# Windowed attention, a gated block and a second block on one core: attention of the last seven pieces by units of two groups, and another order of the work

## The chip, the cores and the metric

The kernel runs on one core of a Trainium2 chip as one program. The metric is the device time of one execution in microseconds (us). The engines are named as in the profile: PE (TensorE matmul), PEld (its weight loads), DVE (VectorE), ACT (ScalarE), POOL (GpSimd) and SP (SyncE, which here only issues DMAs).

## The reference

```python
def _attn_ref(q, k, v):                      # 4 x 8 heads x 576 x 64
    scores = np.matmul(q, k.transpose(0, 1, 3, 2)) / np.sqrt(64)
    rel = pos[:, None] - pos[None, :]
    # heads 0-3: 0 <= rel < 32;  heads 4-7: 0 <= rel < 128 and rel % 4 == 0
    scores = np.where(mask, scores, -1e9)
    attn = np.exp(scores - scores.max(-1))
    return np.matmul(attn / (attn.sum(-1) + 1e-9), v)

def _moe_ref(x, w_gate, w_val, w_out, rms_g):   # 2304 x 512, inner width 1536
    xn = x / np.sqrt(np.mean(x * x, -1) + 1e-06) * rms_g
    g = xn @ w_gate
    return (g / (1 + np.exp(-g)) * (xn @ w_val)) @ w_out

def _moe2_ref(x, w_in, w_out, g_ln):            # inner width 1024
    h = x @ w_in;  solu = h * softmax(h)
    return (layer_norm(solu) * g_ln) @ w_out

def reference(q, k, v, ...):  return _moe2_ref(_moe_ref(rows(_attn_ref(q, k, v))))
```

All inputs and the output are float32. The kernel splits each operand of a large product into a high and a low half in a 32-bit matmul type and adds three products (`mm3`, L889 to L892).

## The kernel before

**Tiling.** The 2304 tokens are cut into nine pieces of 256 (`PIECES`). A piece has four groups of attention work, or five (pieces 4 and 8, counted from 0): two of plain heads, and two of dilated heads or, with five, one kind "both" and two "tail". A group holds 8 blocks of 32 queries with 64 keys each for two heads: 8 score matmuls of 64 by 64, a softmax over 4 slots of 64 keys, 2 transposes, 8 value matmuls of 64 by 64. In the lists each of these 64 by 64 matmuls is issued as x1 and shows as two records in the trace.

**Stages.** Pieces 0 and 1 run first, by `pair` (L453), two groups at a time. Then the gated block starts while weights still come in; for each slice f of 128 of the 1536 inner columns it runs g (gate, 12 matmuls of 512 tokens), vp (value, 12) and y (output, 12), and the weights of a slice are fetched as 64-bit words and made into halves by `prepare` (L341 to L420: shift on ACT, `parts` and `joined` on DVE, `halves` on ACT, `lows` on POOL or DVE). Pieces 2 to 8 take their attention by `attention(t, n)` (L570), one group at a time, between the matmuls of the gated block. Their softmax is `masking` (DVE, L623), `maximum` (DVE, L627), `exps` (ACT, four activations, L632), `norm` (DVE, L636 and L637), `weights` (DVE, L640); then `transposes` (PE, L647), two `turned` (ACT, L304), `values` (PE, L665) and `copy` into x (L308). `rms` (L688) squares and adds on POOL, sums over partitions on PE (`ms`, L787), and spreads the factor (`rs`, L807). After about 335 us a joint stage for the last four pieces follows (a seven-product scheme, L1230), and from about 515 us the second block.

**A burst.** In `scores` (L610) the values of an earlier group are emitted first and then the group's scores, so PE has 16 matmuls of 64 by 64 in a row (32 records). `FOLLOWS` says whose values go with whose scores: those of the group two before (`DISTANCE` 2).

**What sets the order.** Every step is added to `Plan` with its engines, a cost on each, what it needs, what buffers it takes and a due time. `Plan.order` plays these once on the host and emits the steps in that order, so each engine's queue has a fixed order. `NUDGE` adds to due times, `PACE` says after which g of the gated block a group's scores may come. SP's queue holds all loads in one order, and a load whose buffer is still in use holds what is queued behind it. Until plan time 75 the gaps that the plan sees on PE are filled with matmuls on a constant (`fill`, L318).

**Buffers.** `attention` has two buffers for queries and keys, two for values, three for the softmax tile, two for the turned weights, each of one group. Two PSUM banks ("a") serve scores, transposes, values, `ms` and `rs` in turn.

Of the kernel before, what the change touches and what calls it, by code (L numbers as in the profile page):

```python
# [109 lines left out]
NUDGE = {("centred", (1, 1)): -15.5, ("eps", 1): -41.9, ("load_v", (0, 0)): -43.4, ("low", 0, 1): -43.6,  # L110
         ("low", 1, 1): -32.8, ("masking", (2, 0)): 19.9, ("masking", (2, 2)): 39.3, ("masking", (4, 1)): 19.7,
         ("maximum", (1, 1)): -8.1, ("maximum", (2, 0)): 29.4, ("norm", (0, 1)): 8.2, ("out", 2, 1, 1): 45.1,
         ("out", 2, 2, 0): 7.5, ("scale", 0, 1): -35.9, ("scale", 1, 0): -11.5, ("scale", 1, 1): -38.4,
         ("scale", 2, 0): -5.5, ("scale", 2, 1): -25.0, ("scale", 3, 0): -11.4, ("scale", 3, 1): -38.8,
         ("square", 0, 1): -34.9, ("square", 1, 1): -32.9, ("square", 2, 1): -42.3, ("square", 3, 1): -29.9,
         ("total", 3, 0): -9.1, ((1, 0), "lows", 1): 11.0, ((1, 1), "joined", 0): 5.2, ((1, 1), "lows", 2): 10.5,
         ((1, 1), "parts", 2): 7.5, ((1, 11), "fetch", 1): 31.9, ((1, 11), "lows", 0): 19.5,
         ((1, 11), "parts", 0): 22.9, ((1, 2), "parts", 0): 4.7, ((1, 3), "halves", 2): 8.4,
         ((1, 3), "joined", 2): 18.2, ((1, 3), "parts", 1): 11.7, ((1, 4), "joined", 0): 15.8,
         ((1, 4), "lows", 1): -4.6, ((1, 4), "parts", 1): 3.3, ((1, 5), "lows", 2): 36.9, ((1, 5), "parts", 0): 24.1,  # L120
         ((1, 5), "parts", 1): 25.9, ((1, 5), "parts", 2): 25.7, ((1, 6), "parts", 0): 24.5,
         ((1, 7), "joined", 0): 18.7, ((1, 7), "parts", 0): 9.9, ((1, 8), "fetch", 1): 15.9,
         ((1, 8), "parts", 0): 13.8, ((1, 9), "fetch", 1): 18.2, ((1, 9), "parts", 0): 19.0}
# [1771 lines left out]
```

## Time and profile before

| | us |
|---|---|
| median of 3 runs | 727.21 (725.83 to 728.73) |
| the profiled execution | 725.47 |
| its span, first to last instruction | 723.7 |
| PE busy | 712.0 (98%) |
| DVE busy | 495.6 (68%) |
| ACT busy | 367.8 (51%) |
| POOL busy | 130.1 (18%) |

The slices of the page show PE at nine tenths or more in all of 40 slices but the first and the last, and the chain that ended last lies on PE for 90% of the span. Matmuls are pipelined: a record of a matmul of 512 columns lasts 0.39 us, but the next one starts 0.23 us after it. So PE's work is read from start to start, in the list of instructions by time; the columns there are start and duration in us, engine, line, operation, operands and, in brackets, idle time before it and what ended it.

### The profile page before, as it was taken

The page shows a single profiled execution, that of the slowest core. Times are in us where ns is not written, and L with a number is a line of the kernel's source. Part 1 is how long each engine was busy: PE and PEld are TensorE (multiplying, and loading weights), DVE is VectorE, ACT ScalarE, POOL GpSimd, SP SyncE. Part 2 cuts the span into 40 slices and gives each one's busy share as a digit, 9 for nine tenths or more (in the row PEclk, how much of TensorE's full clock was granted, in tenths as well). Part 3 has the DMA queues.
Part 4 walks back from the last instruction along what each step waited for, and adds up shares of the span by engine and source line. Part 5 has one row for each costly group of instructions (what it writes and reads, how often), then busy time and mean ns, then how long its engine had stood idle before and what let it go on. Part 6 is the DMA issues. An engine that isn't in the chain of part 4 may idle for free.

```text
span 723.7 us, 11967 instructions
## 1 busy us (share of the span) xinstructions
PE 712.0 (98%) x4570; PEld 598.2 (83%) x4570; DVE 495.6 (68%) x957; ACT 367.8 (51%) x814; POOL 130.1 (18%) x165
## 2 busy tenths in 40 slices
PE   7999999999999999999999999999999999999997
PEld 5888888899997788788888888888788888888887
DVE  3898997487767767467566666679766677665552
ACT  2896735354545546334655555345464556443440
POOL 0230321333314321210000000024044311001110
PEclk9999999999999999999999999999999999999999
DMA  9998133154468854113211103757032111000001
GB/s 327 404 404 327 50 113 132 57 199 165 167 194 289 316 181 155 81 59 119 86 58 59 59 0 119 279 185 233 30 116 75 58 59 45 30 14 30 30 29 44
DMA packets 42873, 97.24 MB, mean 134 GB/s; under 512 B 4288, under 2 KB 14528, under 8 KB 42816
## 3 DMA queue, kind: packets, MB, share of 16 engines
q1 hardware_dynamic: 41088, 93.33, 37.2%
q10 hardware_dynamic: 1728, 3.15, 1.2%
q8 instruction: 36, 0.59, 0.3%
q14 instruction: 21, 0.17, 0.1%
HBM read 72.87 MB, written 23.59 MB: 133 GB/s over the span
## 4 chain that ended last, share of the span: by engine, by line
PE 90%; DMA 4%; DVE 3%; ACT 1%; SPq 1%; issue 1%; POOL 0%; DVEq 0%; POOLq 0%; ACTq 0%
PE ca L1230 7%; PE y L890 6%; PE y L892 6%; PE y L891 6%; PE o L1627 5%; PE o L1626 5%; PE o L1625 5%; PE g L890 4%; PE vp L890 4%; PE g L891 4%; PE g L892 4%; PE vp L892 4%; PE vp L891 4%; PE cd L1230 2%; PE cb L1230 2%; PE cc L1230 2%
## 5 line engine op out<-in xcount | busy, mean ns | idle before, releaser
L313 POOL TENSOR_TENSOR w<-wf,w 128x512 fp32r<-128x512 f32 (+1 forms) x13 | 22.4, 1733 | 208.2 <-ACT w L304 208.2
L1625 PE MATMUL o<-w,lt 128*128 128x512 f32 (+1 forms) x152 | 58.9, 388 | 0.0
L1627 PE MATMUL o<-w,lt 128*128 128x512 f32 (+1 forms) x152 | 57.6, 379 | 0.0
L1626 PE MATMUL o<-w,lt 128*128 128x512 f32 (+1 forms) x152 | 57.5, 379 | 0.0
L890 PE MATMUL y<-uh,w 128*128 128x512 f32 (+1 forms) x148 | 53.9, 364 | 0.0
L892 PE MATMUL y<-uh,w 128*128 128x512 f32 (+1 forms) x148 | 51.8, 350 | 0.0
L891 PE MATMUL y<-uh,w 128*128 128x512 f32 (+1 forms) x148 | 51.7, 349 | 0.0
L632 ACT ACTIVATE s<-s,nm 128x64 f32<-128x64 f32 x120 | 40.2, 340 | 17.9 <-DVE nm L627 15.1
L924 ACT ACTIVATE u<-g 128x512 f32<-128x512 f32 (+1 forms) x37 | 19.0, 515 | 47.1 <-PE g L892 46.9
L890 PE MATMUL g<-xh,w 128*128 128x512 f32 (+1 forms) x104 | 41.6, 400 | 0.3 <-DVE u L930 0.3
L890 PE MATMUL vp<-xh,w 128*128 128x512 f32 (+1 forms) x100 | 40.2, 402 | 0.0
L772 POOL TENSOR_TENSOR sq<-x 128x256 f32<-128x256 f32 x28 | 17.5, 629 | 125.8 <-ACT x L304 68.8
L892 PE MATMUL g<-xh,w 128*128 128x512 f32 (+1 forms) x104 | 39.3, 378 | 0.0
L891 PE MATMUL g<-xl,w 128*128 128x512 f32 (+1 forms) x104 | 39.3, 378 | 0.0
L892 PE MATMUL vp<-xh,w 128*128 128x512 f32 (+1 forms) x100 | 38.3, 383 | 0.0
L891 PE MATMUL vp<-xl,w 128*128 128x512 f32 (+1 forms) x100 | 38.2, 382 | 0.0
L304 ACT CAST w<-wf 128x512 fp32r<-128x512 f32 (+1 forms) x40 | 28.5, 728 | 18.7 <-DVE wf L366 6.3
L304 ACT ACTIVATE pT<-tp,half 128x256 f32<-128x256 f32 x60 | 25.4, 470 | 23.6 <-PE tp L647 23.5
L934 DVE SCALAR_TENSOR_TENSOR u<-u,vp 128x512 f32<-128x512 f32 (+1 forms) x37 | 21.6, 585 | 18.8 <-PE vp L892 17.9
L930 DVE SCALAR_TENSOR_TENSOR u<-u,g 128x512 f32<-128x512 f32 (+1 forms) x37 | 21.6, 584 | 18.1 <-ACT u L924 17.9
L1593 POOL TENSOR_SCALAR st<-st 128x1 f32<-128x1 f32 x18 | 8.6, 480 | 140.6 <-ACT sq L1584 140.3
L1627 PEld LDWEIGHTS o<-w,lt 128*128 128x128 f32 x152 | 28.6, 188 | 5.3
(283 smaller groups left out, 2069.8 us busy)
## 6 DMA issues: line engine op xcount, KB each, us to landing
raw<-w SPq DMA_DIRECT2D x36, 512.0 KB, 10.2
es<-ec SPq DMA_DIRECT2D x12, 512.0 KB, 4.3
sc<-es SPq DMA_DIRECT2D x12, 512.0 KB, 3.2
vt<-v SPq DMA_DIRECT2D x22, 256.0 KB, 4.3
qk<-qk SPq DMA_DIRECT2D x14, 400.0 KB, 4.0
wo<-w SPq DMA_DIRECT2D x9, 512.0 KB, 5.1
wst<-wo SPq DMA_DIRECT2D x9, 512.0 KB, 3.9
yT<-yo SPq DMA_DIRECT2D x16, 256.0 KB, 2.9
```

The lines of the kernel that those rows point to most:

```text
L304: nc.scalar.copy(dst, src) if scale is None else nc.scalar.mul(dst, src, scale)
L313: ENG[e].tensor_tensor(dst, a, b, ALU.subtract)
L632: nc.scalar.activation(T[s_][:, i], T[s_][:, i], AF.Exp, bias=st["nm"][:, i:i + 1], accum_out=sm[:, i:i + 1])
L890: nc.tensor.matmul(acc, wh, xh, start=first, stop=False)
L891: nc.tensor.matmul(acc, wh, xl, start=False, stop=False)
L892: nc.tensor.matmul(acc, wl, xh, start=False, stop=last)
L930: return lambda e: nc.vector.scalar_tensor_tensor(out=u_of(f), in0=u_of(f), scalar=1.0, in1=T["g", v, f], op0=ALU.add, op1=ALU.mult)
L934: return lambda e: nc.vector.scalar_tensor_tensor(out=u_of(f), in0=u_of(f), scalar=0.5, in1=T["vp", v, f], op0=ALU.mult, op1=ALU.mult)
L1230: nc.tensor.matmul(acc(x), w, y, start=not more and j == 0 and n == 0, stop=j == 1 and n == 2, skip_group_check=True)
L1625: nc.tensor.matmul(o, lt[:, 0, k], w[:, 0], start=(k == 0), stop=False)
L1626: nc.tensor.matmul(o, lt[:, 0, k], w[:, 1], start=False, stop=False)
L1627: nc.tensor.matmul(o, lt[:, 1, k], w[:, 0], start=False, stop=(k == NF2 - 1))
```

## The change

`attention` takes a unit of two groups: `UNITS` pairs the four groups of a piece as (0, 1) and (2, 3), the five as (0), (1, 2) and (3, 4), so 30 groups become 16 units. A burst now holds the values of the unit before and the scores of this unit, up to 32 matmuls in a row; softmax steps work on tiles of 8 slots of 64 keys, `exps` is eight activations, `transposes` four. Of each buffer there is one, twice as wide (values have a second one from piece 5 on). The queue of SP begins with other loads, the `lows` of the first two parts of slice 0 may run on DVE only, `NUDGE`, `PACE` and several costs differ, and with them the order on every engine.

```diff
+NUDGE = {... ('load_v', (0, 0)): 3.07, ('gln',): -100, ((1, 1), 'fetch', 0): 41, ...}
-PACE = {2: [(2, 2), (2, 1), (2, 2), (2, 2)],
+PACE = {2: [(2, 2), (2, 2)],
...
-DISTANCE = 2
-FOLLOWS = {}
-for chain in ((2, 3, 4, 5, 6, 7, 8),):
-    order = [(t, n) for t in chain for n in range(len(GROUPS[t]))]
-    FOLLOWS.update(zip(order[DISTANCE:], order))
+UNITS = [[(0, 1), (2, 3)] if len(gs) == 4 else [(0,), (1, 2), (3, 4)] for gs in GROUPS]
+UNIT_OF = {(t, n): m for t, us in enumerate(UNITS) for m, u in enumerate(us) for n in u}
+CHAIN = [(t, m) for t in range(2, len(PIECES)) for m in range(len(UNITS[t]))]
+FOLLOWS = dict(zip(CHAIN[1:], CHAIN))
...
-    plan = Plan({"qk": 2, "v": 2, ... "s": 3, "pT": 2, ... "vx": 2, ...})
+    plan = Plan({"qk": 1, "v": 1, ... "s": 1, "pT": 1, ... "vx": 1, ...})
...
-            plan.add((key, "lows", n), {"p": pool_, "d": two}, lows(c), ...)
+            plan.add((key, "lows", n), {"d": two} if f == 0 and n < 2 else {"p": pool_, "d": two}, lows(c), ...)
...
-    def attention(t, n, due, needs):
+    def attention(t, m, due, needs):
+        ns = UNITS[t][m]
+        gs, N = [GROUPS[t][n] for n in ns], len(ns)
...
         def load_qk(e):
-            tile_ = new(at, qk, [P, QK_MAX])
-            nc.sync.dma_start(out=tile_[:, 0:w], in_=qk_d[PLACE[K], :, 0:w])
+            T[qk] = at.tile([P, 2, QK_MAX], F32, tag="qk0", name="qk")[:, 0:N]
+            nc.sync.dma_start(out=T[qk][:, :, 0:w], in_=qk_d[at_:at_ + N, :, 0:w].rearrange("g p w -> p g w"))
...
         def scores(e):
-            x = new_bank(sp, [P, 4, 64], "sp")
+            x = new_bank(sp, [P, 8, 64], "sp")
             if K in FOLLOWS:
                 values_of[FOLLOWS[K]](e)
             fill(x.rearrange("p s k -> p (s k)"))
-            for i in range(4):
-                for c in range(2):
...
+            for y in range(N):
+                q = T[qk][:, y]
+                for i in range(4):
+                    for c in range(2):
+                        b = 4 * (i // 2) + 2 * c + i % 2
+                        k0 = 512 + gs[y]["offs"][b]
+                        nc.tensor.matmul(x[64 * c:64 * c + 64, 4 * y + i, :], q[:, 64 * b:64 * b + 64], q[:, k0:k0 + 64],
+                                         start=True, stop=True)
...
         def exps(e):
-            for i in range(4):
+            for i in range(4 * N):
                 nc.scalar.activation(T[s_][:, i], T[s_][:, i], AF.Exp, bias=st["nm"][:, i:i + 1], accum_out=sm[:, i:i + 1])
...
         def transposes(e):
-            for u in range(2):
+            for u in range(2 * N):
                 nc.tensor.transpose(x[:, u], T[s_][:, 2 * u:2 * u + 2, :].rearrange("p r k -> p (r k)"), ident)
...
-                 due={"mask": -9, "ident": -5.5}.get(name, 3))
+                 due={"mask": -7.5, "ident": -6}.get(name, 3))
```

What this does to the queues is shown at four places. The rows are those of one engine's queue in program order: line, operation, output and inputs, size; a line of "..." stands for rows left out.

First PE, where pieces 5 to 8 take turns with the gated block: `pv` is a matmul of values, `sp` of scores, `g`, `vp` and `y` are matmuls of the gated block, `tp` a transpose, `ms` the sum over partitions. Before:

```order
L647 MATMUL tp<-ident,s 128x128 x2
...
L892 MATMUL y_2924<-uh,w_2_546 128x512
L665 MATMUL pv<-pT,vt 64x64 x8
L619 MATMUL sp<-qk 64x64 x8
L890 MATMUL g<-xh,w_0_704 128x512
...
L787 MATMUL ms<-ones,sq 128x1 x2
```

The same piece of work in the changed kernel:

```order
L912 MATMUL g<-xh,w_0_618 128x512
L682 MATMUL pv<-pT,vt 64x64 x16
L626 MATMUL sp<-qk 64x64 x16
L910 MATMUL g<-xh,w_0_618 128x512
...
L912 MATMUL y_2724<-uh,w_2_533 128x512
L807 MATMUL ms<-ones,sq 128x1 x2
...
L662 MATMUL tp<-ident,s 128x128 x4
```

A burst is 32 matmuls instead of 16, and between the burst and the `ms` that follows it stand 24 matmuls of 512 columns instead of 6. Between a unit's burst and its own transposes the shortest such distance is 24 matmuls and one `rs`; all others of two groups are longer.

Second DVE, at the same place; `ec` are sums of weight halves for the joint stage, whose tile comes by DMA, `x<-pv` is `copy`. Before:

```order
L627 TENSOR_REDUCE nm<-s 128x4
L1178 TENSOR_TENSOR ec<-ec 128x256 x4
L308 COPY x<-pv 128x4x64
L623 SCALAR_TENSOR_TENSOR s<-sp,masks 128x256
L627 TENSOR_REDUCE nm<-s 128x4
L636 TENSOR_SCALAR rn<-sm 128x4
```

In the changed kernel:

```order
L1198 TENSOR_TENSOR ec<-ec 128x256 x4
L329 TENSOR_TENSOR uh<-u,uh 128x512
L324 COPY x<-pv 128x2x256
L639 SCALAR_TENSOR_TENSOR s<-sp,masks 128x512
L642 TENSOR_REDUCE nm<-s 128x8
L950 SCALAR_TENSOR_TENSOR u<-u,g 128x512
L954 SCALAR_TENSOR_TENSOR u<-u,vp 128x512
L651 TENSOR_SCALAR rn<-sm 128x8
```

The `ec` sums still stand ahead of a `copy`; one row of each kind now serves two groups.

Third SP, at the head of its queue. Before:

```order
L461 DMA qkv<-v 128x2x512
L1777 DMA masks<-mask 128x704
L457 DMA qkv<-qk 128x2x800 x2
L1777 DMA ident<-ident 128x128
L457 DMA qkv<-qk 128x2x896
L461 DMA qkv<-v 128x2x512
```

In the changed kernel:

```order
L1797 DMA gln<-gln 128x8
L473 DMA qkv<-qk 128x2x800
L1797 DMA masks<-mask 128x704
L473 DMA qkv<-qk 128x2x800
L1797 DMA ident<-ident 128x128
L473 DMA qkv<-qk 128x2x896
L473 DMA qkv<-qk 128x2x800
L477 DMA qkv<-v 128x2x512 x2
```

Values of the first two groups moved behind all four loads of queries and keys. Up to the load of the third tile of weights (`raw_2`) the queue carries the same bytes as before, but for a load of 2 KB that moved behind it.

Fourth DVE at the end of the attention of piece 0: `r<-ms` is the first step after the sum over partitions, `raw` are weight words. Before:

```order
L508 TENSOR_TENSOR s<-s,rn 128x512
L362 TENSOR_SCALAR raw_1_301<-raw_1_301 128x512
L794 TENSOR_SCALAR r<-ms 128x2
L366 SCALAR_TENSOR_TENSOR wf<-raw_1_301 128x512
L802 TENSOR_SCALAR rd<-ident,r 128x128 x2
L362 TENSOR_SCALAR raw_2_317<-raw_2_317 128x512
```

In the changed kernel:

```order
L524 TENSOR_TENSOR s<-s,rn 128x512
L378 TENSOR_SCALAR raw_1_307<-raw_1_307 128x512
L378 TENSOR_SCALAR raw_2_336<-raw_2_336 128x512
L814 TENSOR_SCALAR r<-ms 128x2
L329 TENSOR_TENSOR w_0_351<-wf,w_0_351 128x512
L822 TENSOR_SCALAR rd<-ident,r 128x128 x2
```

The row on the third tile of weights moved ahead of `r<-ms`, and a `lows` of slice 0 came from POOL to stand behind it.

## Rows read from the trace of the kernel before

**Rows 1.** Stretches: start:end, length, PE busy, granted clock, DMA share, GB/s.
```profile
0.00:39.69 39.69, 33.32 (x419) 0.96 0.97 369
57.57:316.00 258.43, 257.21 (x2179) 1.00 0.48 165
```

**Rows 2.** Instructions by time, PE: a burst of values and scores.
```profile
87.73 0.39 PE L891 MATMUL g<-xl,w 128*128 128x512 f32 x1
87.96 0.39 PE L892 MATMUL g<-xh,w 128*128 128x512 f32 x1
88.28 0.69 PE L665 MATMUL pv<-pT,vt 128*64 128x64 f32 x16
...
89.36 0.50 PE L890 MATMUL vp<-xh,w 128*128 128x512 f32 x1
89.69 0.39 PE L891 MATMUL vp<-xl,w 128*128 128x512 f32 x1
```

**Rows 3.** Instructions by time, PE: a burst of values alone.
```profile
301.03 0.40 PE L892 MATMUL y<-uh,w 128*128 128x512 f32 x1
...
301.97 0.50 PE L890 MATMUL g<-xh,w 128*128 128x512 f32 x1
302.31 0.40 PE L891 MATMUL g<-xl,w 128*128 128x512 f32 x1
```

**Rows 4.** Instructions by time, PE: piece 0, scores and values back to back.
```profile
17.30 1.15 PE L481 MATMUL sp<-qkv 128*64 128x64 f32 x32 [0.32 <-DMA qkv<-qk]
18.29 1.10 PE L537 MATMUL pv<-xp,qkv 128*64 128x64 f32 x32
```

**Rows 5.** Instructions by time, PE: two transposes in a row, and eight.
```profile
154.88 0.38 PE L647 MATMUL tp<-ident,s 128*128 128x128 f32 x2
...
155.22 0.28 PE L891 MATMUL g<-xhl,w 128*128 128x256 f32 x1
...
536.07 1.03 PE L1606 MATMUL tp<-ident,he 128*128 128x128 f32 x8
...
537.17 0.40 PE L1553 MATMUL hd<-w,w 128*128 128x512 f32 x1
```

**Rows 6.** Instructions by time, DVE and PE: a wait of PE.
```profile
232.50 1.88 DVE L1178 TENSOR_TENSOR ec<-ec 128x256 f32<-128x256 f32 x4 [2.13 <-DMA ec<-pw]
...
234.29 0.60 DVE L308 COPY x<-pv 128x256 f32<-128x256 f32 x1
...
233.42 0.40 PE L892 MATMUL g<-xh,w 128*128 128x512 f32 x1
...
235.04 0.58 PE L787 MATMUL ms<-ones,sq 128*128 128x1 f32 x4 [1.22 <-DVE x L308]
```

**Rows 7.** The start, by time; then the DMA issue of 15.1 to 15.4 us.
```profile
11.37 1.15 PE L481 MATMUL sp<-qkv 128*64 128x64 f32 x32 [0.22 <-DMA qkv<-qk]
...
24.65 0.16 DVE L794 TENSOR_SCALAR r<-ms 128x2 f32<-128x2 f32 x1
...
39.69 0.36 PE L890 MATMUL g<-xh,w 128*128 128x256 f32 x1 [0.34 <-DVE u L930]
...
raw<-w SPq DMA_DIRECT2D x1, 512.0 KB, 8.7
```

**Rows 8.** Softmax: DVE of 512 columns and small ones, by time; ACT's group.
```profile
15.78 0.69 DVE L485 TENSOR_REDUCE nm<-sp 128x8 f32<-128x512 f32 x1
...
17.19 0.16 DVE L504 TENSOR_SCALAR rn<-sm 128x8 f32<-128x8 f32 x1
17.39 0.20 DVE L505 RECIPROCAL rn<-rn 128x8 f32<-128x8 f32 x1
...
L632 ACT ACTIVATE s<-s,nm 128x64 f32<-128x64 f32 x120 | 40.2, 340 | 17.9 <-DVE nm L627 15.1
```

**Rows 9.** A stretch with the lower clock, columns as in rows 1.
```profile
31.00:35.00 4.00, 4.00 (x23) 0.57 1.03 406
```

**Rows 10.** SP's queue by time: the load behind the first scores.
```profile
58.61 0.33 SPq L598 DMA_DIRECT2D qk<-qk  x1
```

More of the change, by code (lines that the diff above doesn't have):

```diff
@@ L560, in pair @@
         plan.add(step("weights"), {"d": 0.7}, weights, [step("norm")], uses=[s_], due=due)
[L561 removed]
+        plan.add(step("transposes"), {"t": 0.66}, transposes, [step("weights")], takes=[(banks[1], tp)], uses=[s_], due=due)
         for r in range(2):
@@ L694, in attention @@
         step = lambda x: (x, K)
-        def ahead(x):
-            return [(x, (t, n - 1))] if n else [(x, (t - 1, len(GROUPS[t - 1]) - 1))] if t > 2 else []
-        plan.add(step("load_qk"), {"s": 1.1}, load_qk, needs, takes=[("qk", qk)], due=DUE_THIRD + 50 * (t - 2) + 10 * n - 8, after=ahead("load_v"))
-        plan.add(step("load_v"), {"s": 0.7}, load_v, needs + ([("load_v", (5, 1))] if v_tag == "vx" and K != (5, 1) else []),
-                 takes=[(v_tag, vt)] + [("x", ("vx",))] * (K == (5, 1)), uses=[("vx",)] * (v_tag == "vx"), due=DUE_THIRD + 50 * (t - 2) + 10 * n - 6, after=[step("load_qk")])
+        before = [FOLLOWS[K]] if K in FOLLOWS else []
@@ new lines, in attention @@
+        plan.add(step("load_qk"), {"s": 2.6 if N == 2 else 1.6}, load_qk, needs, takes=[("qk", qk)],
+                 due=DUE_THIRD + 50 * (t - 2) + 20 * m - 8, after=[("load_v", x) for x in before])
+        plan.add(step("load_v"), {"s": 1.9 if N == 2 else 1.2}, load_v,
+                 needs + ([("load_v", first_vx)] if v_tag == "vx" and K != first_vx else []),
+                 takes=[(v_tag, vt)] + [("x", ("vx",))] * (K == first_vx), uses=[("vx",)] * (v_tag == "vx"),
+                 due=DUE_THIRD + 50 * (t - 2) + 20 * m - 6, after=[step("load_qk")])
@@ L726, in attention @@
             needs_, takes_, uses_ = for_values(K)
-            plan.add(step("values"), {"t": 0.75}, values, needs_, takes=takes_, uses=uses_, due=due)
-        plan.add(step("copy"), {"d": 0.5, "a": 0.5}, copy,
-                 [step("values") if K not in LEADS else ("scores", LEADS[K])] + ([("copy", (t, 0))] if n else []) +
-                 ([("copy", (t - 1, 0))] if t in (6, 8) and n == 0 else []),
+            plan.add(step("values"), {"t": 0.27 + 0.465 * N}, values, needs_, takes=takes_, uses=uses_, due=due)
+        cost = 0.7 if N == 2 and g["kind"] != "tail" else 0.5 * N
+        plan.add(step("copy"), {"d": cost, "a": cost}, copy,
+                 [step("values") if K not in LEADS else ("scores", LEADS[K])] + ([("copy", (t, 0))] if m else []) +
+                 ([("copy", (t - 1, 0))] if t in (6, 8) and m == 0 else []),
                  uses=[pv, x_key(t)], due=due)
@@ L849, in rms @@
                      square(k), [("values", (t, source[k] // 2))] if stays else
-                     [("copy", (t, n)) for n in range((whole[k] // 2 if first else whole[k]) + 1)],
+                     [("copy", (t, m)) for m in range(UNIT_OF[t, whole[k]] + 1)],
                      takes=[("sq", ("sq", t, k))], uses=[("pvs", (t, source[k] // 2))] if stays else [xk], due=due,
@@ L1784, in tile_attention_glu_solu @@
         else:
-            for n in range(len(GROUPS[t])):
-                attention(t, n, DUE_THIRD + 10 * n if t == 2 else -1 if t < 5 else -3, [("g", *PACE[t][n], 0)])
+            for m in range(len(UNITS[t])):
+                attention(t, m, DUE_THIRD + 20 * m if t == 2 else -1 if t < 5 else -3, [("g", *PACE[t][m], 0)])
         rms(t, DUE_NORM[t] if t < 2 else DUE_THIRD + 40 if t == 2 else -1, t < 2)
```

182 lines of the change are left out of this document (100 added, 82 removed), and 8 rows, old and new, of tables (PACE, plan).

## The prediction

> **What bounds the kernel now.** First the stretches of the span by engine [rows 1]: until 39.69 us PE works for 33.32 us, much of it on the filling constant, while the DMA queues are full (a share of 0.97, 369 GB/s). From 57.57 to 316 us, where the attention of pieces 2 to 8 runs, PE is busy for 257.21 of 258.43 us at a granted clock of 1.00, and nearly all that is missing is one wait. So the time is the start plus the sum of PE's work; another engine costs something only where it makes PE wait. Next the list of PE's instructions by time, read from start to start, gives the price of each kind of work [rows 2 to 5]. Then comes the one wait [rows 6]: at 233.42 us PE starts its last matmul ahead of `ms`, and `ms` starts at 235.04 after 1.22 us of idleness. It waits for `copy` on DVE (234.29), which stood behind `ec`, which waited 2.13 us for a DMA. Last, the start by time [rows 7].
>
> **The bursts.** Two neighbouring 512-column matmuls start at 87.73 and 87.96, a step of 0.23 us. From 87.96 to the second matmul behind a burst of 32 records (89.69) it is 1.73 us; without two steps the burst costs 1.27 us [rows 2]. A burst of values alone has 16 records: 301.03 to 302.31 is 1.28 us, less 0.46 is 0.82 us [rows 3]. So 16 more records cost 0.45 us, and 0.82 - 0.45 = 0.37 us is left for going over to 64 by 64 and back, whatever the number. Independently, in piece 0 bursts stand back to back, and 32 records take 18.29 - 17.30 = 0.99 us [rows 4], a little more than 2 x 0.45 = 0.90.
>
> Before there are 31 bursts for the 30 groups of pieces 2 to 8: the first with the scores of two groups, 28 of values and scores, two of values alone. That is 29 x 1.27 + 2 x 0.82 = 38.5 us for 960 records. After there are 17: scores alone (32 records), 11 of 64, four of 48 around the units of one group, values alone (32). By rows 2 and 3 these cost 2 x 1.27 + 11 x 2.17 + 4 x 1.72 = 33.3 us; by the dearer rate of rows 4 they cost 2 x 1.27 + 11 x 2.26 + 4 x 1.77 = 34.5 us. It saves 4.0 to 5.2 us. I take 4.4, nearer to the lower end, because the rate of rows 4 was measured on a long run of such records and a burst of 64 is a long run.
>
> The Trainium skill, "TensorEngine Tiling (Array Packing)", section Tiling Modes, says that changing the tiling mode drains TensorE; it gives no price. The traced remainder of 0.37 us is of that kind. By the same page's Performance Considerations, each matmul has an overhead of some 60 cycles and a short one costs as much as one of 60 columns; were that all, the price would go by records alone and this term would be 0 instead of 4.4. That is rival B.
>
> **Transposes** go from two to four in a row. Two take 155.22 - 154.88 = 0.34 us less a step, and eight take 537.17 - 536.07 = 1.10 less a step of 0.23; with a 256-column step of about half of 0.23 for the first, both come to about 0.11 us each [rows 5]. No fixed part shows: 0, and at most some tenths in all.
>
> **The wait at `ms`.** Between burst and `ms` stood 6 matmuls, 6 x 0.23 = 1.4 us; now it is 24, 5.5 us. The cover grows by 4.1 us, against a wait of 1.22 us [rows 6]. `ec` still stands ahead of a `copy`; its DMA would have to come 2.9 us later, relative to PE, for PE to wait. I take -1.2 us; 0 if the wait comes back elsewhere.
>
> **The start.** Moving the values of the first two groups behind the queries and keys takes a load of 128 x 2 x 512 words, 512 KB, from ahead of the second pair's queries and keys: at 369 GB/s [rows 1] 1.4 us. Its scores stood at 11.37 us after a wait of 0.22 us for that load [rows 7]; they come earlier, by about a microsecond at most. But DVE's row on `raw_2` now stands ahead of `r<-ms`, which began at 24.65. The weight load issued at 15.1 to 15.4 us landed 8.7 us later, at about 23.9 [rows 7], behind the same bytes as now. So of that microsecond only 24.65 - 23.9 = 0.75 us can come through, and DVE's work behind that load takes most of it. A wait of 0.34 us at 39.69 on DVE's `u` [rows 7] may go, since the rows behind it were put in another order. Against it, the `lows` of slice 0 go from POOL to DVE at the place where DVE is the busiest. A `lows` of 512 columns is one such step of DVE, 0.69 us by the nearest row of that width [rows 8], and costs that if it ends up on the chain to `u`. The ends are -(0.75 + 0.34) = -1.1 and +0.7; I take -0.4 us, a part of what can come through.
>
> **Costed at nothing.** DVE and ACT do the same softmax elements in fewer (DVE) or as many (ACT) instructions; they saved nothing for PE, whose queue was full. Single buffers for queries, keys and values put a unit's loads behind the burst before; the cover is a unit's worth of gated block, many times the few microseconds of a load. The other weight fetches, `NUDGE` and `PACE` move work between full stretches of PE. Without cover each is a wait on PE, which is rivals A and C.
>
> **Sum.** -4.4 - 1.2 - 0.4 = -6.0 us. On the profiled execution's own 725.47 that is 719.5; the median of the runs is 727.21, 1.7 above, so I predict **721.2 us**. With the ends: -5.2 - 1.2 - 1.1 = -7.5 gives 719.7, and -4.0 + 0 + 0.7 = -3.3 gives 723.9. On top, executions differ by a microsecond or two either way.
>
> **Rivals.**
> A, the slower one: a unit's own chain becomes longer than its cover. Between a unit's burst and its `tp` lie at least 24 matmuls (5.5 us) and one `rs`. The chain is three DVE steps of 512 columns (0.69 us each), eight `exps` of 0.34 us, and two small DVE steps of 0.16 and 0.20 us [rows 8]: 2.07 + 2.72 + 0.36 = 5.15 us. With four hand-overs between engines at 0.15 us (from the end of `copy`, 234.29 + 0.60, to `ms` at 235.04 [rows 6]) it is 5.75: about even at the shortest place, and covered where the distance is longer. What speaks for it is that one set of buffers leaves no second unit to run ahead, and that DVE has other rows between these steps; if DVE's queue is a few rows of 0.69 us late, PE waits at every burst. 15 bursts make it slower than before by over 0.5% from 0.64 us of waiting each (721.2 + 9.6 = 730.8). Chance 0.05 for that, 0.13 for a mild form of 0.16 to 0.64 us each (723.6 to 730.8).
> B, the change doesn't do what it says: the price goes by records. 725.47 - 1.6 + 1.7 = 725.6 us. Against it, 32 records cost 1.27 and 16 cost 0.82, not 0.64 [rows 2, 3]. Chance 0.06.
> C, a load is held in SP's queue. There is such a place now: a load of queries and keys was issued only at 58.61 us, when scores had freed its buffer, with weight loads behind it [rows 10]. Some weights now come in another order, into tiles that pieces 0 and 1 use. A late load of 512 KB costs PE 1.4 us at the rate of rows 1, two 2.8: 724.0 us. Chance 0.04.
> D, the clock. From 31 to 35 us the granted clock was 0.57 on average, so much of it at 1.2 instead of 2.4 GHz [rows 9]; PE had gone through a row of short matmuls and waits before it. Now most of that falls on filling. If the lower clock falls on the gated block behind 39.69 us, 4.00 x 0.43 = 1.7 us more work must be done: 722.9 us. Chance 0.07.
>
> **How the numbers follow.** About 0.5%, 3.6 us, is what a measurement can tell from no change: faster is below 723.6, slower above 730.8. The forecast has 0.65, and with D faster has 0.72. The mild A, B and C give 0.23 for the same, the strong A 0.05 for slower. The range begins at 717.5, where all terms are at their favourable ends and the run is a good one, and goes to 726.0, which takes in B, C, D and the lower part of the mild A; about 0.05 of strong A, half of mild A and a tail of the forecast below are left out, under 0.2.
>
> **What would show it.** In the new trace: bursts of 64 records at 2.2 us from start to start, and 1.27 for the first and last; no idle time at `ms`; second scores about 10.4 us, `r<-ms` about 24.3, PE's gated block without a gap from about 39.3. Idle time ahead of `tp`, `pv` or `sp` on ACT or DVE would show A, on a DMA C; bursts of 2.5 us B; a granted clock under 1.00 behind 40 us D. The forecast would be wrong above all if the burst's fixed part isn't paid once per burst, or if one PE wait per unit appears.

## The result and the profile after

The changed kernel takes 717.09 us (median of four runs, 716.19 to 717.8), the kernel before, timed beside it, 726.75; the ratio is 0.9863 (95% interval 0.9839 to 0.9887). In a later series of five rounds it was 0.9865 (0.9849 to 0.9881). The forecast was 721.2 us with a range from 717.5: the direction was right, the gain of 9.7 us is 1.6 times the 6.0 forecast, and the time lies 0.4 us under the range.

The profiled execution of the changed kernel took 717.14 us. The head of its page:

```profile
span 715.1 us, 11752 instructions
PE 706.7 (99%) x4561; PEld 597.1 (83%) x4561; DVE 485.6 (68%) x891; ACT 361.8 (51%) x775; POOL 125.7 (18%) x159
```

The span is 8.6 us shorter than before. Three positions on PE divide it: the first g of the second 256 tokens (before at 39.69 [rows 7]), the first `ca` of the joint stage, which takes place after the attention, and the last matmul.

| stretch | before, us | after, us | difference |
|---|---|---|---|
| start to the first g of the second 256 tokens | 39.69 | 37.53 | -2.2 |
| from there to the first `ca` (336.83; 328.06) | 297.14 | 290.53 | -6.6 |
| first `ca` to the last matmul (719.73; 711.59) | 382.90 | 383.53 | +0.6 |
| last matmul to the end of the span | 4.0 | 3.5 | -0.5 |

A burst of 64 records in the list of PE's instructions by time (start, duration, engine, line, operation, operands), the answer to [rows 2]:

```profile
128.83 0.39 PE L912 MATMUL y<-uh,w 128*128 128x512 f32 x1
129.15 1.15 PE L682 MATMUL pv<-pT,vt 128*64 128x64 f32 x32
130.13 1.10 PE L626 MATMUL sp<-qk 128*64 128x64 f32 x32
131.16 0.50 PE L910 MATMUL y<-uh,w 128*128 128x512 f32 x1
131.50 0.39 PE L911 MATMUL y<-uh,w 128*128 128x512 f32 x1
```

From 128.83 to 131.50 it is 2.67 us; less two steps of 0.23 the burst costs 2.21 us, where two bursts of [rows 2] cost 2.54. The 0.33 us between them is the price that each joined pair saves, and 14 bursts fewer are 4.6 us by this pair.

Where the kernel before waited for `ec` [rows 6], DVE now finds the data there. These are rows of DVE by time, with no wait in brackets:

```profile
225.66 1.79 DVE L1198 TENSOR_TENSOR ec<-ec 128x256 f32<-128x256 f32 x4
227.79 1.80 DVE L1198 TENSOR_TENSOR ec<-ec 128x256 f32<-128x256 f32 x4
```

PE has no idle time at all in the stretch of the attention (start:end, length, busy time of PE, PEld, DVE, ACT and POOL, granted clock, DMA share, GB/s):

```profile
55.42:310.00 254.58, 254.58 (x2191) 221.21 (x2190) 175.60 (x326) 129.62 (x388) 62.93 (x74) 1.00 0.49 172
```

The start, the answer to [rows 7], first on PE, then on DVE and POOL:

```profile
7.29 1.15 PE L497 MATMUL sp<-qkv 128*64 128x64 f32 x32
9.13 1.15 PE L497 MATMUL sp<-qkv 128*64 128x64 f32 x32
...
25.85 0.70 PE L827 MATMUL rs<-rd,ones 128*128 128x256 f32 x2 [0.61 <-DVE rd L822]
...
33.44 1.06 PE L827 MATMUL rs<-rd,ones 128*128 128x256 f32 x2
...
37.53 0.36 PE L910 MATMUL g<-xh,w 128*128 128x256 f32 x1
```

```profile
23.61 0.43 DVE L378 TENSOR_SCALAR raw<-raw 128x512 uint32<-128x512 uint32 x1 [0.33 <-DMA raw<-w]
23.96 0.15 DVE L814 TENSOR_SCALAR r<-ms 128x2 f32<-128x2 f32 x1
25.32 0.48 DVE L822 TENSOR_SCALAR rd<-ident,r 128x128 f32<-128x128 f32 x2 [0.61 <-POOL r L817]
31.36 1.57 DVE L822 TENSOR_SCALAR rd<-ident,r 128x128 f32<-128x128 f32 x2 [0.26 <-POOL r L817]
...
31.37 1.28 POOL L329 TENSOR_TENSOR xl<-xp,xh 128x512 fp32r<-128x512 f32 x1
```

The scores stand 1.9 and 2.2 us earlier, `r<-ms` only 0.69 us (24.65 before), since the row on `raw_2` ahead of it waited for its load; the first `rs` stands 1.72 us earlier (27.57 before). Between the last two lies `rd`, which takes 0.48 us. In the kernel before it took 1.48, with a step of POOL beside it, both times:

```profile
26.03 1.48 DVE L802 TENSOR_SCALAR rd<-ident,r 128x128 f32<-128x128 f32 x2 [0.60 <-POOL r L797]
33.28 1.50 DVE L802 TENSOR_SCALAR rd<-ident,r 128x128 f32<-128x128 f32 x2 [0.59 <-POOL r L797]
...
25.96 1.27 POOL L313 TENSOR_TENSOR w<-wf,w 128x512 fp32r<-128x512 f32 x1
33.21 1.28 POOL L313 TENSOR_TENSOR w<-wf,w 128x512 fp32r<-128x512 f32 x1
```

POOL's step is a `lows` of slice 0. The new theory of the start is thus: 0.7 us come from the order of loads, 1.0 us because the first `lows` no longer runs on POOL beside `rd`. The last 0.4 us lie behind the first `rs`, where among other things the wait of 0.34 us for `u` [rows 7] is gone.

### The profile page after: what moved, and what is told of

It is laid out like the page before. It is cut to its first block, busy times and chain, and to the rows that moved or that the text cites. A ratio compares the mean times of both kernels' runs of the same rounds, so it can differ in the third digit from the quotient of the medians.

```text
span 715.1 us, 11752 instructions
## 1 busy us (share of the span) xinstructions
PE 706.7 (99%) x4561; PEld 597.1 (83%) x4561; DVE 485.6 (68%) x891; ACT 361.8 (51%) x775; POOL 125.7 (18%) x159
## 4 chain that ended last, share of the span: by engine, by line
PE 88%; DVE 4%; DMA 4%; issue 1%; ACT 1%; POOL 1%; SPq 1%; DVEq 0%; ACTq 0%; POOLq 0%
PE ca L1250 7%; PE y L910 5%; PE y L912 5%; PE y L911 5%; PE o L1647 5%; PE o L1645 5%; PE o L1646 5%; PE g L910 4%; PE vp L910 4%; PE g L911 4%; PE vp L912 4%; PE g L912 4%; PE vp L911 4%; PE pv L682 2%; PE cd L1250 2%; PE cc L1250 2%
## 5 line engine op out<-in xcount | busy, mean ns | idle before, releaser
L329 POOL TENSOR_TENSOR w<-wf,w 128x512 fp32r<-128x512 f32 (+1 forms) x12 | 19.8, 1658 | 196.4 <-ACT w L320 196.4
L792 POOL TENSOR_TENSOR sq<-x 128x256 f32<-128x256 f32 x28 | 19.7, 713 | 127.2 <-DVE x L324 65.4
L320 ACT CAST uh<-u 128x512 fp32r<-128x512 f32 (+1 forms) x37 | 19.8, 536 | 28.8 <-DVE u L954 28.5
L1647 PEld LDWEIGHTS o<-w,lt 128*128 128x128 f32 x152 | 28.6, 188 | 5.4
L1645 PEld LDWEIGHTS o<-w,lt 128*128 128x128 f32 x152 | 28.6, 188 | 4.8
```

The source lines that it names most:

```text
L320: nc.scalar.copy(dst, src) if scale is None else nc.scalar.mul(dst, src, scale)
L329: ENG[e].tensor_tensor(dst, a, b, ALU.subtract)
L1645: nc.tensor.matmul(o, lt[:, 0, k], w[:, 0], start=(k == 0), stop=False)
L1647: nc.tensor.matmul(o, lt[:, 1, k], w[:, 0], start=False, stop=(k == NF2 - 1))
```

## The experiments

Each kernel is the one before or the changed one with the edit shown. Where only the place or the engine of steps differs, the list of steps is edited after it is put in order:

```diff
-        for at_, _, name, e in plan.play():
+        for at_, _, name, e in rearranged(plan.play()):   # applies MOVE and FORCE
```

All of them in one table; "g" is the first g of the second 256 tokens and `ca` the first of the joint stage. Times without an interval are single runs; the kernel before took 727.61 beside the first four and 728.17 beside the next four.

| run | us | ratio to before (95%) | g | `ca` |
|---|---|---|---|---|
| before_lows_dve | 724.52 | | 36.70 | 336.14 |
| before_qk_first | 725.88 | | 38.81 | 337.20 |
| before_both | 725.25 | | 37.72 | 336.93 |
| after_lows_pool | 718.13 | | 38.31 | 329.17 |
| after_v_first | 718.56 | | 39.08 | 329.85 |
| after_xl_dve | 716.18 | | 36.53 | 327.55 |
| after_split | 723.58 | | 37.39 | 334.89 |
| after_ahead | 719.73 | | 36.75 | 331.53 |
| before_again | 726.63 | 1.0003 (0.9992 to 1.0014) | 39.71 | 338.32 |
| before_ec_later | 728.95 | 1.0031 (1.0012 to 1.005) | 40.02 | 341.11 |
| before_all | 724.95 | 0.9986 (0.9965 to 1.0007) | 37.98 | 337.95 |
| after_again | 716.42 | 0.9865 (0.9849 to 0.9881) | 37.51 | 328.22 |
| after_old_start | 718.52 | 0.9889 (0.987 to 0.9908) | 39.49 | 330.02 |
| after_xl_dve_timed | 716.98 | 0.9877 (0.9859 to 0.9895) | 39.15 | 330.31 |
| after_xl_fewer | 717.01 | 0.9876 (0.9856 to 0.9895) | 36.66 | 328.80 |
| after_fewer | 716.90 | 0.9883 (0.986 to 0.9905) | 36.45 | 327.41 |
| before_light | 724.35 | 0.9966 (0.9952 to 0.998) | 40.47 | 336.21 |
| before_light_start | 721.95 | 0.9934 (0.9907 to 0.996) | 37.82 | 333.55 |

### The start: two causes, each alone

```diff
+FORCE = {((1, 0), 'lows', 0): 'd', ((1, 0), 'lows', 1): 'd'}
+MOVE = [(((1, 0), 'lows', 0), 'behind', ('diag', 0)), (((1, 0), 'lows', 1), 'behind', ('diag', 1))]
```

> The kernel before, with one edit: the two `lows` of the first two weight tiles run on DVE, each behind the `rd` rows that follow it, and not on POOL; all other steps keep their places. Theory P (the two engines hinder each other): the two `rd` rows last 1.48 us in the kernel before because POOL works on `lows` from 25.96 us on beside them, and 0.48 us without; so `rd` takes about 0.5 us, `rs` of piece 0 starts at about 26.6 instead of 27.57, and the first g of the second 256 tokens starts 0.5 to 1.5 us before 39.69. Rival D (as in the prediction: DVE is the busiest engine there): a `lows` costs DVE 0.69 us on the chain, and that g starts at 39.7 to 40.4.

```diff
+MOVE = [(('load_v', (0, 0)), 'behind', ('load_qk', (1, 1))), (('load_v', (0, 1)), 'behind', ('load_qk', (1, 1)))]
```

> The kernel before, with one edit: the loads of the values of the first two groups pairs stand behind all four loads of queries and keys in SP's queue. Theory L (as in the prediction): scores come 1.4 to 2 us earlier, but the row on `raw_2` and the weight rows around it hold DVE, so that `r<-ms` moves from 24.65 to 23.9 at the earliest and the first g of the second 256 tokens from 39.69 by at most 0.75 us. Rival S (the whole shift goes through): that g starts about 1.7 us or more earlier, at 38.0 or before.

Both edits together:

> The kernel before, with both edits: the two `lows` on DVE behind the `rd` rows, and the values loaded behind the queries and keys. If the two causes P and L are what shortened the start, the first g of the second 256 tokens, at 39.69 before and at 37.53 in the changed kernel, starts at 37.6 to 38.4. If it stays above 38.8, the order of the rows of DVE and ACT (silu ahead, the first half of g ahead of `rs`) makes the larger part.

Both causes are seen in the rows, but not all in the sizes expected. With `lows` on DVE both `rd` took 0.48 us. From `r<-ms` to the end of the second `rd` it is 10.1 to 10.2 us in the five traces of this kernel with `lows` on POOL and 8.1 us in the four with them on DVE (those of the section on the wait below included): 1.0 us at each `rd`, whenever the loads came. The order of loads is less sharp. `r<-ms` stood at 23.75 to 25.83 us in the five traces with the old order and at 23.68 to 24.11 in the four with the new one, on average 24.81 against 23.89, so a shift of 0.7 or 0.9 us between two single executions is within what the loads vary by themselves.

In before_lows_dve the g stood at 36.70, 3.0 us earlier where 0.5 to 1.5 were expected; 0.9 us of it is the first loads, which came sooner in this execution though their order was not changed, and 2.0 is `rd`. With queries and keys first, `r<-ms` and g moved by 0.9 us each, where at most 0.75 was expected. With both edits g stood at 37.72, as expected, but that is not the sum of the two: the second `rd` ended at 31.79 us, as early as in before_lows_dve (31.87), and PE reached `rs` only at 33.20 (31.92 there). The granted clock between 31 and 35 us was 0.77, against 1.00 in before_lows_dve and 0.57 in the kernel before; what sets it is open. So the place of g carries about a microsecond that is not the edit's.

Beside the execution of before that is shown above (336.83), `ca` moved by only -0.7, +0.4 and +0.1 us. PE by time, in before_lows_dve:

```profile
36.70 0.36 PE L904 MATMUL g<-xh,w 128*128 128x256 f32 x1 [0.52 <-DVE u L944]
...
229.25 0.41 PE L661 MATMUL tp<-ident,s 128*128 128x128 f32 x2 [1.83 <-DVE s L654]
234.39 0.58 PE L801 MATMUL ms<-ones,sq 128*128 128x1 f32 x4 [0.67 <-DVE x L322]
```

The 1.22 us of idle time at `ms` [rows 6] has become 0.61 at 56 us, 1.83 and 0.67 at 229 and 234. In before_both PE waits at the same places, and 0.55 us more at 250:

```profile
229.24 0.41 PE L661 MATMUL tp<-ident,s 128*128 128x128 f32 x2 [1.68 <-DVE s L654]
234.43 0.58 PE L801 MATMUL ms<-ones,sq 128*128 128x1 f32 x4 [0.72 <-DVE x L322]
```

This looks as if whoever comes sooner waits longer. A second execution of the kernel before, in the section on the wait, shows that it is not so.

### The same start in the changed kernel

```diff
+FORCE = {((1, 0), 'lows', 0): 'p', ((1, 0), 'lows', 1): 'p'}
```

> The changed kernel, with one edit: the two `lows` of the first two weight tiles run on POOL again, at the places that they have in the order. Theory P: the first is beside `rd` again, which lasts 1.5 instead of 0.48 us; the first g of the second 256 tokens starts 0.7 to 1.5 us behind 37.53, and the total is 0.7 to 1.5 us longer. Rival D: DVE is relieved of 1.4 us; that g starts at 37.5 or earlier.

```diff
+MOVE = [(('load_v', (0, 0)), 'ahead', ('gln',)), (('load_v', (0, 1)), 'behind', ('load_qk', (1, 0))), (('gln',), 'ahead', ('rmsg',))]
```

> The changed kernel, with one edit: the values of the first two group pairs are loaded where the kernel before loads them (the first ahead of all else, the second behind three loads of queries and keys). Theory L: the scores start about 2 us later, at 9.2 and 11.2 us, `r<-ms` moves from 23.96 to about 24.6, and the first g of the second 256 tokens starts 0.4 to 0.8 us behind 37.53. Rival S: the whole shift of about 2 us goes through, and it starts at 39.2 or later.

With `lows` on POOL the g came 0.78 us later, as expected, but by other rows: the first `lows` now stood ahead of POOL's `r`, and the first `rd` kept its 0.48 us. What suffered was a small DVE row that takes 0.17 us elsewhere [rows 8], while POOL worked from 21.41 to 22.68:

```profile
21.41 1.27 POOL L343 TENSOR_TENSOR w<-wf,w 128x512 fp32r<-128x512 f32 x1 [20.11 <-ACT w L334]
...
21.53 1.18 DVE L534 TENSOR_SCALAR rn<-sm 128x8 f32<-128x8 f32 x1
```

It ended 0.03 us after POOL did. Later the second `lows` on POOL (30.97 to 32.26 us) stood ahead of the second `r`. The second `rd` ended 1.7 us later (34.63; 32.93 in the changed kernel); that g came only 0.78 us later goes with the granted clock between 31 and 35 us, 1.00 here and 0.57 there: from the end of `rd` to g it was 3.68 us instead of 4.60. `ca` came 1.1 us later (329.17), of which 0.31 is a wait of one `tp` for DVE. With the values first, `r<-ms` moved to 24.57 as expected, and g to 39.08, which is more than the 0.4 to 0.8 us of theory L and less than rival S; the second `rd` ended 0.35 us later (33.28), and the rest was PE, whose filling ran until 35.57 us. `ca` came 1.8 us later, 0.25 of it a wait at `tp`. In the changed kernel, then, the start does reach the attention's end. Both edits at once, timed:

> The changed kernel, unchanged, beside the next two for comparison: ratio 0.985 to 0.988 to the kernel before.

> The changed kernel with the start of the kernel before in two respects: values loaded ahead of the queries and keys, and the two `lows` on POOL. The first g of the second 256 tokens then starts 1.5 to 2.5 us behind 37.53. Theory T (in the changed kernel nothing behind the start waits for a DMA, so all of it reaches the end): 1.5 to 2.5 us more than the changed kernel, a ratio to the kernel before of 0.989 to 0.991. Rival G (given back behind the start, as in the three variants of the kernel before): within 0.5 us of the changed kernel.

```profile
39.49 0.36 PE L924 MATMUL g<-xh,w 128*128 128x256 f32 x1
...
330.02 1.52 PE L1264 MATMUL ca<-w,w 128*128 128x512 f32 x6
```

From g to `ca` it is 290.53 us, as in the two traces of the changed kernel (290.53 and 290.71). The time is 718.52 against 716.42 us, 2.1 us more: theory T, though the ends of the two intervals overlap.

### The wait at `ec`

> The kernel before, unchanged, once more with a profile. Theory W: the wait of DVE's `ec` rows for their DMA around 225 to 235 us follows the DMA and not PE, so that its size differs between executions; PE's idle time from 220 to 240 us, 1.22 us in the profile shown, comes out anywhere from 1 to 3 us, and the span with it. Rival: it is 1.2 us again, and the 1.7 us between that profiled execution and the median has another place.

The kernel before, unchanged, waits differently in another execution (PE by time):

```profile
231.29 0.41 PE L647 MATMUL tp<-ident,s 128*128 128x128 f32 x2 [1.70 <-DVE s L640]
236.53 0.58 PE L787 MATMUL ms<-ones,sq 128*128 128x1 f32 x4 [0.77 <-DVE x L308]
...
338.32 1.52 PE L1230 MATMUL ca<-w,w 128*128 128x512 f32 x6
```

That is 2.47 us of idle time, not 1.22, and the span is 725.2 us, not 723.7. This execution took 726.98 us, near the median; the one shown of before was a short one, and the wait accounts for most of the difference.

It also changes what the three variants of the start mean. Their waits behind 220 us (2.50, 2.27 and 2.95 us in the order of the table) are about those of this execution, which has the old start. Beside it they reach `ca` 2.2, 1.1 and 1.4 us sooner, and their times, each of a single run, lie 0.7 to 2.1 us under the median of before in this series (726.57). The loads of `ec` came sooner with the start: the third was issued at 220.05 us in before_lows_dve and at 222.18 here. So the runs do not show that the earlier start made the waits longer; most of it came through, as far as single executions can tell.

```diff
+MOVE = [(('ecomb', 8), 'behind', ('maximum', (6, 1))), (('estore', 8), 'behind', ('ecomb', 8)),
+        (('ecomb', 9), 'behind', ('masking', (6, 2)))]
```

> The kernel before, with one edit: two of the `ec` sums, which wait for a DMA around 225 and 232 us on DVE, stand behind the softmax and `copy` rows that PE waits for. Theory W: no idle time of PE from 220 to 240 us any more; the time falls by that idle time, 1.2 us of the profile shown or more in other executions (ratio 0.9965 to 0.9985). Rival: the wait turns up again at a later row (`prod`, `ms`), and the ratio is 1.000.

The expectation failed, and the kernel is slower. The two waits are gone and a longer one stands at the next sum but one, first on DVE, then on PE:

```profile
248.42 2.91 DVE L1192 TENSOR_TENSOR ec<-ec 128x256 f32<-128x256 f32 x4 [4.91 <-DMA ec<-pw]
...
253.01 0.66 PE L661 MATMUL tp<-ident,s 128*128 128x128 f32 x2 [3.84 <-DVE s L654]
```

The sums have two buffers: a load, the sum, its store, and only then the next load but one. A sum that is put off puts off the store and with it that load. From g to `ca` it is 301.09 us, without the wait 297.25, 1.5 more than in a kernel without waits (295.74, below); the granted clock was 0.73 between 250 and 255 us, behind the wait. With the edits of the start added:

> The kernel before, with the three edits together: `lows` on DVE behind the `rd` rows, values loaded behind queries and keys, and the two `ec` sums later; bursts stay as they were. With the first two edits alone the gated block started 2 us earlier, and PE gave the whole of it back in front of `tp` and `ms` at 229 and 234 us. Theory W: with the `ec` sums out of the way the 2 us stay, and the first `ca` comes at 333 to 334 us instead of 336.83; ratio about 0.995. Rival: something else, such as the gated block's weights, sets the time there, and `ca` stays at 336 or later.

`ca` stayed at 337.95 us, with 2.72 us of idle time at 249.85; the ratio is not told apart from 1. So these sums could not be moved out of the way. But beside before_ec_later, which puts off the same sums, the two edits of the start took 4.0 us off (728.95 to 724.95, intervals apart): there the start came through. Instead, the loads were made short, which leaves out part of the data:

```diff
-                nc.sync.dma_start(out=flat(room()), in_=plain_w[fp, X].rearrange("p i m -> p (i m)"))
+                w = 1024 if q < NF1 // 2 + 2 else 16
+                nc.sync.dma_start(out=flat(room())[:, 0:w], in_=plain_w[fp, X].rearrange("p i m -> p (i m)")[:, 0:w])
```

> The kernel before with one part left out: the last four of the six loads of halves for the `ec` sums bring only the first 16 of 1024 words (the sums then work on what the tile held), so that these loads are short; stores and sums stay. Theory W: PE has no idle time of over 0.3 us between 220 and 260 us; 1.2 to 2.5 us less than the kernel before, ratio about 0.997. Rival: PE waits there for something else, and the time stays.

> The same with the two edits of the start (two `lows` on DVE behind the `rd` rows, values loaded behind queries and keys). Theory W: the shorter start, given back at the `ec` waits before, now stays: 1 to 2.5 us less than the kernel with the short loads alone, the first `ca` at 332 to 334 us. Rival: it is given back elsewhere, and both kernels take the same time within 0.5 us.

Here theory W is borne out, but for its half sentence that the start had been given back before. PE has no wait between 60 and 330 us in either, and the time falls to 724.35 and then to 721.95 us. In before_light_start:

```profile
37.82 0.36 PE L904 MATMUL g<-xh,w 128*128 128x256 f32 x1 [0.19 <-DVE u L944]
...
333.55 1.52 PE L1245 MATMUL ca<-w,w 128*128 128x512 f32 x6
```

From g to `ca` it is 295.73 us with the short start and 336.21 - 40.47 = 295.74 without. Without the long `ec` loads the start is passed on whole.

### The price of a burst

One more matmul of 512 columns, on the filling constant, in the middle of each burst or ahead of it:

```diff
             if K in FOLLOWS:
+                # after_ahead: the matmul stands here
                 values_of[FOLLOWS[K]](e)
+                # after_split: it stands here instead
+                nc.tensor.matmul(x.rearrange("p s k -> p (s k)"), seed[:, 0:1].to_broadcast([P, P]),
+                                 seed.to_broadcast([P, 512]), start=True, stop=True)
```

> The changed kernel with one more matmul of 512 columns over the whole array (on the filling constant) in each of the 15 bursts of pieces 2 to 8, between its values and its scores. Theory F (a fixed price for going over to 64 by 64 and back): each split costs one matmul step, about 0.23 us, and 0.3 to 0.37 us more; 15 x 0.55 to 0.60 = 8.3 to 9.0 us. Rival B (price by records alone): 15 x 0.23 = 3.5 us, as with the matmul ahead of the burst.

> The changed kernel with the same 15 matmuls of 512 columns, but ahead of each burst, behind another matmul over the whole array. By every theory 15 x 0.23 = 3.5 us; the difference to the kernel with them in the middle is 15 x 0.30 to 0.37 = 4.5 to 5.5 us by theory F, and 0 by rival B.

The same burst in both, PE by time:

```profile
129.67 0.39 PE L914 MATMUL y<-uh,w 128*128 128x512 f32 x1
129.99 1.15 PE L684 MATMUL pv<-pT,vt 128*64 128x64 f32 x32
131.07 0.39 PE L619 MATMUL sp<-seed 128*128 128x512 bf16 x1
131.40 1.15 PE L628 MATMUL sp<-qk 128*64 128x64 f32 x32
...
132.81 0.39 PE L913 MATMUL y<-uh,w 128*128 128x512 f32 x1
```

```profile
129.03 0.39 PE L914 MATMUL y<-uh,w 128*128 128x512 f32 x1
129.26 0.39 PE L618 MATMUL sp<-seed 128*128 128x512 bf16 x1
...
131.93 0.39 PE L913 MATMUL y<-uh,w 128*128 128x512 f32 x1
```

Ahead, from y to y, it is 2.90 us: 2.67 and one step of 0.23. In the middle it is 3.14, 0.24 us more. So a cut in a burst has a price of its own, and rival B is out. It is less than the 0.30 to 0.37 expected; the matmul in the cut is a bf16 one and not one of the gated block's, which may be why, but no run shows that. In all, `ca` came 6.8 us later than in the changed kernel with the matmuls in the middle, where 8.3 to 9.0 were expected, and 3.5 us later with them ahead, as expected.

The joined bursts themselves are the better measure for the change. All bursts of before_light and of the changed kernel that stand between matmuls of 512 columns, costed as in [rows 2], take 0.81 to 0.82 us with 16 records, 1.27 to 1.29 with 32, 1.74 with 48 and 2.20 to 2.22 with 64. That is 0.46 us for every 16 records and 0.35 for every burst, and 14 x 0.35 = 4.9 us.

### Faster still?

```diff
+FORCE = {('low', 0, 0): 'd', ('low', 1, 0): 'd'}
+MOVE = [(('low', 1, 0), 'behind', ('diag', 1))]
```

> The changed kernel, with one edit: the two low halves `xl` of piece 0, which POOL computes from 28.52 and from 31.37 us, run on DVE, the second behind the `rd` rows of piece 1. Theory P: the second `rd` lasts about 0.5 us instead of 1.57, since nothing runs on POOL beside it; `rs` of piece 1 starts at 32.4 to 32.9 instead of 33.44, and the first g of the second 256 tokens up to 1 us before 37.53. Rival D: DVE gets 1.4 us more work on its chain, and that g starts 0.3 to 1 us later.

> The changed kernel with the two `xl` of piece 0 on DVE, timed: one look had the second 256 tokens start 1.0 us earlier (36.53 instead of 37.53). Theory T: 0.8 to 1.2 us less than the changed kernel. Rival G: within 0.3 us of it.

The second `rd` took 0.48 us in both, as expected, but in the profiled execution of the timed series `r<-ms` came 1.3 us later (25.12; 23.86 in the single run), and then PE stood in the way: the 16 filling matmuls ahead of the second `rs` ran until 35.05 us, 1.3 us after `rd`, at a granted clock of 0.73 between 31 and 35 us (columns as in the stretch of the attention above).

```profile
35.05 1.06 PE L841 MATMUL rs<-rd,ones 128*128 128x256 f32 x2
...
31.00:35.00 4.00, 4.00 (x27) 3.24 (x27) 3.39 (x9) 4.00 (x8) 1.09 (x1) 0.73 0.93 366
```

Fewer of them, with and without that edit:

```diff
+                if name == ("spread", 1):
+                    filling[0] = 6
```

> The changed kernel with two edits: the two `xl` of piece 0 on DVE, and 6 instead of 16 filling matmuls ahead of the second `rs`. Where the granted clock fell between 31 and 35 us, the 16 took 2.87 us (30.57 to 33.44) and 3.06 us, and PE was late for `rd` by 0.5 and 1.3 us. Theory C (the filling at the lower clock holds the start): the second 256 tokens start at 36.3 to 37.0 and the time is 0.5 to 1.2 us less than the changed kernel's 716.4. Rival: less filling lets the clock fall longer, on the gated block, and nothing or up to 1 us is lost.

> The changed kernel with one edit: 6 instead of 16 filling matmuls ahead of the second `rs`, `xl` on POOL as it was. `rd` ends at 32.93 there and `rs` starts at 33.44: theory C gives at most 0.5 us; the rival 0 to 1 us more.

In both traces g stood about 1 us earlier than in the changed kernel (36.66 and 36.45), and the clock was 1.00 up to 40 us; with fewer filling matmuls alone:

```profile
32.81 0.70 PE L827 MATMUL rs<-rd,ones 128*128 128x256 f32 x2 [1.58 <-DVE rd L822]
...
36.45 0.38 PE L910 MATMUL g<-xh,w 128*128 128x256 f32 x1
37.18 0.39 PE L911 MATMUL g<-xl,w 128*128 128x256 f32 x1 [0.34 <-DVE xl L329]
...
31.00:35.00 4.00, 2.42 (x19) 2.14 (x17) 3.63 (x7) 3.27 (x7) 1.92 (x3) 1.00 1.01 396
```

Only this first matmul gained the microsecond, for the next one waits for `xl` on DVE. The third stood at 37.61 and 37.40 us, against 37.85 in the changed kernel, so 0.24 and 0.45 us were gained. The medians are 717.01 and 716.90 us against 716.42 and 717.09 for the changed kernel, and the intervals overlap. None of these can be called faster.

## Why the prediction was wrong

**The bound** was read rightly: PE is saturated behind 40 us, and the time followed PE's work and PE's waits.

**The bursts** were right in mechanism and size. 4.4 us were taken between 4.0 and 5.2; 4.6 came by one joined pair, 4.9 by the mean of all bursts. Without any `ec` wait it is 295.73 us from g to `ca` in bursts of one group and 290.53 in the changed kernel: 5.2 us, in which some tenths of other work are included. Transposes came out at nothing, as said: two cost 0.22 us beyond the steps around them (74.85 us in before_light), four 0.44 (63.75 us in the changed kernel).

**The wait at `ms`** is the first mis-sized term: 1.2 us, from one execution. In another one of the same kernel it was 2.5, and taking away the loads behind it was worth 2.2 us of the median (726.58 to 724.35). A row `[1.22 <-DVE x]` behind a DVE row `[2.13 <-DMA ec<-pw]` [rows 6] is a wait for a transfer, whose length differs from execution to execution; it should have had a range upwards. That it is gone was right, but not for the reason given. The prediction counted on the 24 matmuls that now cover the way to `ms`. In the trace DVE doesn't wait in the first place, because the load comes earlier. These are the loads of the sum at 232.50 us [rows 6] and of the same one in the changed kernel, at 227.79 us, by SP's queue:

```profile
227.24 0.33 SPq L1173 DMA_DIRECT2D ec<-pw  x1
...
221.07 0.32 SPq L1193 DMA_DIRECT2D ec<-pw  x1
```

Before, the load was issued 3.1 us before DVE came to the sum (230.37), in the changed kernel 6.7 us. Its buffer was free sooner, perhaps because an earlier sum, which POOL finished only at 222.01 us, now runs on DVE; no run tests that, nor whether the longer cover alone would have been enough.

**The step from span to median** failed with it. 1.7 us were added because the profiled execution of before was that much under its median. That difference was mostly the longer wait in the usual execution, which the change takes away: after it, the profiled 717.14 and the median 717.09 are the same. The same wait was thus counted as gone with 1.2 us and kept with 1.7.

**The start** is the second mis-sized term, by size the larger one, and one part of it had the wrong sign: -0.4 was taken between -1.1 and +0.7, and -2.2 came. The scores came 1.9 and 2.2 us earlier, not by a microsecond at most, but as said `raw_2` let little of it through: 0.69 us at `r<-ms`, against the bound of 0.75. That `lows` goes from POOL to DVE was priced as a loss of up to 0.69 us; it gained 1.0, since `rd` is no longer held. The trace of before had the two rows of 1.48 and 1.50 us, three times what the same row takes alone, and POOL's row beside each; they were not compared. The Trainium skill states the rule ("SBUF — State Buffer", Who interferes with whom): VectorE in some forms, which copies and operations with a scalar can enter, and GpSimd take a shared pair of ports exclusively, and the one that comes second waits until the first has finished. The rows here agree: a DVE row of 0.17 us took 1.18 and ended 0.03 us behind POOL's step.

**Adding** the terms was not the mistake. In timed kernels 726.58 us fall to 724.35 without the long `ec` loads, to 721.95 with the shorter start, and to 717.09 or 716.42 with the bursts and the rest of the change: 2.2 + 2.4 + 4.9 to 5.5. The sizes above give 4.6 to 4.9 for the bursts, 2.2 to 2.5 for the wait, 2.2 for the start and 0.5 for a shorter end behind the last matmul, whose cause was not looked into: 9.5 to 10.1 us, where 9.7 were measured. The forecast was short by 1.8 us in the start, by 1.0 to 1.3 in the wait, by 0.2 to 0.5 in the bursts and by the 0.5 at the end, which it did not have.

**The rivals.** A did not come: PE has no wait at `tp`, `pv` or `sp` in the changed kernel. The shortest cover is indeed used up, as worked out (5.75 against 5.5 us): in four variants of the changed kernel one `tp`, at 195 to 196 us, waited 0.20 to 0.64 us for DVE's `s`. In after_v_first:

```profile
195.81 0.63 PE L676 MATMUL tp<-ident,s 128*128 128x128 f32 x4 [0.25 <-DVE s L669]
```

B fell with the cut bursts. What the Trainium skill says of an overhead of each matmul ("TensorEngine Tiling (Array Packing)", Performance Considerations) is not tested here, since the matmuls of all bursts have 64 columns. C was not seen in the changed kernel; a load of queries and keys 0.65 us late showed in one variant of it, after_xl_fewer. D did not come: the lower clock stayed in the same stretch, 0.57 between 31 and 35 us [rows 9] and 0.57 after, mostly under filling. Behind the attention two waits for DVE's `st` in the second block, 0.25 and 0.40 us where there was one of 0.38, are part of the 0.6 us lost there. It is not a loss of the change: in after_again the stretch behind the first `ca` takes 382.95 us, as before, with the first of these waits alone.

```profile
508.01 0.50 PE L1572 MATMUL hb<-w,yh 128*128 128x512 f32 x1 [0.25 <-DVE st L1580]
530.00 0.50 PE L1572 MATMUL hb<-w,w 128*128 128x512 f32 x1 [0.40 <-DVE st L1580]
```

## What to carry to other kernels

Before a difference between two kernels is put down to an edit, look at a second execution of each. Here the shorter start seemed to be lost at the wait for `ec`, because the one trace of before had a wait half as long as usual; a second trace of the same kernel had the longer wait with the old start. Where a position moves with the loads or with the clock, compare stretches that hold only the edited rows: from `r<-ms` to the end of `rd` the edit was worth 2.0 us each time, while g moved by up to a microsecond for other reasons. Compare each row with the same row elsewhere in the trace; one that takes three times as long beside another engine's step names a cause to test. And a wait that ends on a DMA has a length only for the one execution that was profiled, so keep it out of both the sum and the step from span to median, or in both with the same range.

## What the runs showed of the hardware that was not expected

- A DVE row with a scalar operand, small or large, stood still while POOL worked on a tensor of 512 columns: 0.17 became 1.18 us and 0.48 became 1.48 to 1.57. Each ended 0.03 to 0.29 us behind POOL's step.
- Changing from full matmuls to those of 64 by 64 and back has a price that does not depend on their number: 0.82, 1.28, 1.74 and 2.21 us for bursts of 16, 32, 48 and 64 records, so 0.35 us beside 0.46 for every 16 records; 0.24 us for a cut with one bf16 matmul in it.
- The filling meant to keep the clock up ran at the lower clock itself in some executions: 16 matmuls took 2.87 us (30.57 to 33.44) at a granted clock of 0.57 between 31 and 35 us in the changed kernel, and 1.97 us at 1.00 in after_xl_dve, after_ahead and after_lows_pool. With 6 in their place both traces showed 1.00, so the number is not shown to be what sets it. What does is open, and the time did not change.
